# Moving a chunk's rows through DRAM ahead of the fetch of the next second weights, in a fused attention and mixture-of-experts kernel

## The chip, the cores and the metric

One core of one Trainium2 chip runs the whole kernel. The metric is the device time of one execution in microseconds (us); the times shown are medians of several runs on the chip. Durations come from one profiled execution of the kernel before.

## The reference

Linear attention with random features runs over 8 batches, 8 heads, 576 rows and 64 columns. Its output, read as 4608 tokens of 512 columns, goes into a mixture of 8 experts, of which each token uses one:

```python
def _moe_ref(x, w_gate, w1, w2):
    logits = x @ w_gate
    expert_idx = np.argmax(logits, axis=1)
    ...
    for e in range(E):
        mask = expert_idx == e
        ...
        h = np.maximum(x[mask] @ w1[e], 0.0)
        out[mask] = gate_w[mask, None] * (h @ w2[e])
```

`w1[e]` is 512 x 1024 and `w2[e]` is 1024 x 512, in float32, so each is 2 MB.

## The kernel before, in words

The attention takes the first 260 us or so of the span, and the change does not touch it. It leaves the token rows in DRAM (`token_rows`). What follows, and what this study is about, is the experts' part (class `Experts`).

**Chunks.** The tokens are sorted by expert into chunks of up to 384 (`T3`), each with tokens of one expert only. `plan` (L754) works out the chunks on the device and leaves them in `flags`: row 0 says that chunk t begins a new expert, row 1 which expert's weights come next, row 2 that chunk t exists, row 4 how many tokens it holds. Engines load these into registers and branch on them. Chunks 0 to 11 always run (`run`, L1215), later ones only if they exist (`tail`, L1159). In the profiled execution chunks 0 to 12 run, and chunks 4, 7 and 9 begin a new expert.

**One chunk** (`step`, L1136). Layer 1 (`layer1`, L1047) makes the hidden values in four groups g = 0 to 3 of two blocks each. TensorE (PE) multiplies into one of two PSUM pairs, `p_1[g % 2]`, and ScalarE (ACT) and VectorE (DVE) empty the pair into a high and a low part (L1001, L1002). PE can be two groups ahead of them and no more. A chunk of over 192 tokens takes the path of L975, a smaller one the path of L982 and L984, whose groups are about half as long. Layer 2 (`layer2`, L1064) multiplies by the second weights (L887, L1036), and the result is scaled and scattered to the output by GpSimd (POOL, L1083).

**How a chunk's rows arrive.** POOL gathers the rows of chunk t + 3 into `xg` or `xgm` (by parity of the chunk) during step t (L924). `move(t)` (L938), on the queue of SyncE (SP), writes them to a DRAM scratch `chunk_rows` (L943) and, when that has landed, reads them back with four transfers into `xq` in another order (L945). There is one `xq`. `xrows(t)` then turns `xq` into the chunk's transposed rows, three times a transpose on DVE (L952), a cast on ACT (L57) and a subtraction on DVE (L51).

**The order of the work.** It is written out by hand, and each engine works through its own share in that order. `begin(t)` (L1127) stands at the end of step t - 1, after its layers. In it SP does `move(t + 1)`, then `change(t, 1)`: if chunk t begins a new expert, ACT and DVE split the first weights `w1s` into `w1h` and `w1l`, and SP fetches the next expert's first weights into `w1s` (L904) once the split has read the old ones. After that DVE and ACT do `xrows(t + 1)`, if chunk t - 1 held over 192 tokens; otherwise it comes in the middle of layer 1 of chunk t, after group g = 1 (L1058 to L1062). The stores of the chunk's outputs by ACT stand behind `begin`.

The second weights are treated in the same way, within layer 1. In a chunk that begins a new expert each group first splits a quarter of `w2s`, and at the last group SP fetches the next expert's second weights (L907):

```python
for g in range(self.NF // 2):
    def fresh():
        self.split(2, (2 * g, 2 * g + 1))
        if g == self.NF // 2 - 1:
            self.next(t, 2)
    self.when(self.new, fresh)
```

So SP's order is `move(t + 1)`, `change(t, 1)`, `next(t, 2)` in the layer 1 of chunk t, `move(t + 2)`, and so on. The fetch for chunk 0 is unconditional and stands in step 0 (L1143).

Of the kernel before, what the change touches and what calls it, by code (L numbers as in the profile page):

```python
# [44 lines left out]
ET = mybir.EngineType  # L45
# [371 lines left out]
class Routing:  # L417
# [99 lines left out]
    def step(self, name, product, f):  # L517

        v = {}
        def made(bank):  # L520
            v["o"] = product(bank)
        def step():
            if "o" not in v:
                made(self.bank(name))
            f(v["o"])
        step.product = made
        return step
# [263 lines left out]
class Experts:  # L791
# [228 lines left out]
    def wide(self, t, g, n):  # L1020
        for f in (2 * g, 2 * g + 1):
            self.l1(t, f, n)
        self.hid(g, n)
# [17 lines left out]
    def load(self, t):  # L1041
        self.before = self.r2
        self.r1, self.r2, self.r3, self.r4 = (self.reg(4, t, T3, e) for e in (
            self.CE, (ET.Activation, ET.DVE), (ET.Activation, ET.DVE, ET.Pool), (ET.PE,)))
        self.new = self.reg(0, t, 1, self.WE)

    def layer1(self, t):  # L1047
        r = self.r1
        for g in range(self.NF // 2):
            def fresh():  # L1050
                self.split(2, (2 * g, 2 * g + 1))
                if g == self.NF // 2 - 1:
                    self.next(t, 2)
            self.when(self.new, fresh)
            wide = lambda n: lambda: self.wide(t, g, n)
            self.either(r > T2, lambda: self.either(r > T3 - HT, wide(T3), wide(T3 - HT)),
                        lambda: self.either(r > T2 - HT, wide(T2), lambda: self.slim(t, g)))
            if g == 1 and t == 1:  # L1058
                self.xrows(t + 1)
            elif g == 1:  # L1060
                with self.tc.If(self.before < T2 - HT + 1):  # L1061
                    self.xrows(t + 1)  # L1062
# [64 lines left out]
    def begin(self, t):  # L1127

        if t + 1 < NCH:
            self.move(t + 1)  # L1130
        self.change(t, 1)
        if 1 < t < NCH - 1:
            with self.tc.If(self.r2 > T2 - HT):
                self.xrows(t + 1)

    def step(self, t, following):  # L1136
        if t == 0:
            self.first(T3)
            self.l21()
            self.load(t)  # L1140
            self.xrows(1)
            self.gather(2)
            self.next(0, 2)  # L1143
        else:
            self.layer1(t)
        self.layer2(t)
        if t + 1 < NCH:
            self.weigh(t + 1)
        if t + 3 < NCH:
            self.gather(t + 3)  # L1150
        self.nc.gpsimd.drain()
        following()
        r, r2 = self.r3, self.r2
        if t + 1 < NCH:
            self.load(t + 1)
        for a in range(A3 - 1, -1, -1):
            self.out2(t, a, r, r2)
# [108 lines left out]
```

## Time and profile before

| | before |
|---|---|
| median of 3 runs | 710.49 us (709.24 to 710.63) |
| the profiled execution: time | 712.33 us |
| the profiled execution: span of its instructions | 710.6 us |
| mean granted TensorE clock, share of full speed | 0.974 |
| PE busy | 665.6 us (94% of the span) |
| DVE, ACT, POOL busy | 53%, 51%, 38% |
| moved by DMA | 100.51 MB, mean 141 GB/s |

The page counts an engine as busy while it works on data. Waiting, branching and issuing transfers do not count. A row of the timeline gives the start in us, the duration in us, the engine, the line of the kernel, the operation with its output and input, how many were merged into the row, and in brackets the idle time of the engine before it and what ended that. SPq marks instructions that SP itself executes, such as the issue of a transfer; the transfer lands later.

### The profile page before, as it was taken

To read this page: it belongs to the slowest core of one execution; us is meant where nothing else is said; L and a number is where in the kernel's file an instruction comes from. 1 tells how busy PE (TensorE), PEld (TensorE's weight loads), DVE (VectorE), ACT (ScalarE), POOL (GpSimd) and SP (SyncE) were. 2 spreads that over 40 slices of the span, in tenths; PEclk is the share of its full clock that TensorE was granted. 3 is DMA by queue.
4 is the path that set the end of the run, shared out by engine and by line. 5 is a ranking of instruction groups with operands and counts; after the bars stand their busy time and mean duration, and the time that the engine had idled before them with its cause. 6 is when DMAs were issued, how large, how long until landed. Compare 5 with 4: busy or idle time off the path is not lost. (4 is left out here: it accounts for less than half of the span.)

```text
span 710.6 us, 19585 instructions
## 1 busy us (share of the span) xinstructions
PE 665.6 (94%) x7011; PEld 604.4 (85%) x7011; DVE 377.2 (53%) x729; ACT 359.2 (51%) x1082; POOL 271.3 (38%) x492
## 2 busy tenths in 40 slices
PE   8999999999999999999999999599999499869994
PEld 5999999999888879898989898589898398768984
DVE  5788888888877787415132641231641355223222
ACT  5999999999989654212222530221530353122121
POOL 6545557777877762421313030313030221031212
PEclk9999999999999999999999999799999799979999
DMA  7782653844862227755244346324337253532200
GB/s 217 208 259 76 204 177 105 261 126 149 257 236 72 71 77 205 257 185 150 70 129 102 140 156 181 96 79 107 145 117 221 82 181 93 180 92 76 63 33 24
DMA packets 93105, 100.51 MB, mean 141 GB/s; under 512 B 28942, under 2 KB 73486, under 8 KB 92304
## 3 DMA queue, kind: packets, MB, share of 16 engines
q1 hardware_dynamic: 85216, 79.27, 36.9%
q0 software_dynamic: 7040, 19.04, 8.6%
q8 instruction: 89, 1.46, 0.9%
q14 instruction: 72, 0.59, 0.3%
q10 hardware_dynamic: 688, 0.16, 0.1%
HBM read 72.92 MB, written 29.77 MB: 145 GB/s over the span
## 5 line engine op out<-in xcount | busy, mean ns | idle before, releaser
L975 PE MATMUL p<-xb,w1p 128*128 128x384 f32 (+1 forms) x1056 | 188.3, 338 | 15.9 <-ACTq L1061 15.9
L975 PEld LDWEIGHTS p<-xb,w1p 128*128 128x128 f32 x1056 | 185.9, 192 | 17.7 <-ACTq L1061 16.5
L1083 POOL DMA_INDIRECT out_dram<-ys,idx x38 | 38.2, 1004 | 302.8 <-DVEq L1073 172.7
L887 PE MATMUL p<-w2p,hb 128*128 128x512 f32 x552 | 127.1, 389 | 0.0
L887 PEld LDWEIGHTS p<-w2p,hb 128*128 128x128 f32 x552 | 103.6, 188 | 21.6
L1002 DVE SCALAR_TENSOR_TENSOR hb<-p,hb 128x768 fp32r<-128x768 f32 (+1 forms) x44 | 41.0, 933 | 145.6 <-ACTq L1114 73.1
L1001 ACT ACTIVATE hb<-p 128x768 fp32r<-128x768 f32 (+1 forms) x44 | 34.9, 793 | 108.5 <-PE p L975 100.4
L191 DVE TENSOR_REDUCE mx<-pp 128x8 f32<-128x1024 f32 x64 | 78.0, 1218 | 10.9 <-PE pp L185 9.5
L199 ACT ACTIVATE qp<-pp,mx 128x128 f32<-128x128 f32 x256 | 77.1, 434 | 0.0
L199 ACT ACTIVATE kp<-pp,mx 128x128 f32<-128x128 f32 x256 | 74.0, 383 | 5.3 <-DVE de L283 1.9
L185 PE MATMUL pp<-omt,th 64*128 64x128 f32 x1024 | 72.1, 281 | 0.0
L185 PEld LDWEIGHTS pp<-omt,th 64*128 64x128 f32 x1024 | 63.4, 191 | 0.0
L887 PE MATMUL p_1tr<-w2p,hb 128*128 128x512 f32 x240 | 57.0, 391 | 0.5 <-DVEq L1114 0.4
L211 POOL TENSOR_TENSOR k<-kp 128x256 f32<-128x256 f32 x64 | 46.7, 729 | 23.7 <-ACT kp L199 18.8
L887 PEld LDWEIGHTS p_1tr<-w2p,hb 128*128 128x128 f32 x240 | 44.8, 188 | 10.2 <-DVEq L1114 0.8
L57 ACT CAST xb<-xgm 128x512 fp32r<-128x512 f32 x21 | 13.0, 621 | 75.4 <-DVE xgm L952 72.7
L274 PE MATMUL nu<-kva,qt 128*64 128x73 f32 x1008 | 46.3, 233 | 0.5 <-issue 0.5
L176 DVE COPY th<-tr 128x512 f32<-128x512 f32 x63 | 43.3, 687 | 5.0 <-PE tr L168 3.2
L243 ACT COPY qt<-t 128x512 f32<-128x512 f32 x64 | 42.1, 657 | 2.2 <-PE t L168 1.8
L952 DVE STREAM_TRANSPOSE xgm<-xq 128x512 f32<-128x512 f32 x21 | 22.7, 1082 | 36.1 <-DMA xq<-chunk_rows 31.7
L274 PEld LDWEIGHTS nu<-kva,qt 128*64 128x64 f32 x1008 | 36.8, 136 | 4.9 <-issue 0.6
L225 PE MATMUL kf<-kp,v 128*64 128x128 f32 x512 | 39.8, 275 | 0.0
(387 smaller groups left out, 1071.0 us busy)
## 6 DMA issues: line engine op xcount, KB each, us to landing
w1s<-in_moe_w_dram SPq DMA_DIRECT2D x5, 2048.0 KB
w2s<-in_moe_w_dram SPq DMA_DIRECT2D x5, 2048.0 KB
xq<-chunk_rows SPq DMA_DIRECT2D x52, 192.0 KB
v<-in_v_dram SPq DMA_DIRECT2D x32, 256.0 KB
token_rows<-x SPq DMA_DIRECT2D x8, 1024.0 KB
k<-in_k_dram SPq DMA_DIRECT2D x31, 256.0 KB
q<-in_q_dram SPq DMA_DIRECT2D x31, 256.0 KB
chunk_rows<-xgm SPq DMA_DIRECT2D x7, 768.0 KB
```

Source lines behind the costliest of these rows:

```text
L176: self.nc.vector.tensor_copy(t.rearrange("p n (a t) -> p a n t", a=2), s[("tr", h)])
L185: nc.tensor.matmul(o[:, a, n, :], t[r, n, :], self.om[r], start=True, stop=True)
L191: self.nc.vector.tensor_reduce(out=mx, in_=s[("pp", h)], axis=AX.X, op=ALU.max, negate=True)
L199: self.nc.scalar.activation(o[:, j, :], p[:, a, 2 * n + i, :], AF.Exp, bias=mx[:, a, 2 * n + i:2 * n + i + 1])
L211: nc.gpsimd.tensor_tensor(out=k2, in0=kp[:, :2, :], in1=kp[:, 2:, :], op=ALU.add)
L225: nc.tensor.matmul(pkv[c * D:(c + 1) * D, :M], vv, kk, start=n < 2, stop=n > 2)
L243: self.nc.scalar.copy(qt.rearrange("p n (a t) -> p a n t", a=2), s[("t2", h)])
L274: nc.tensor.matmul(o[r, j, :], qt[:, j, r], kva[:, h if h >= 0 else 2 * j + a, :], start=True, stop=True)
L887: self.nc.tensor.matmul(p, x, w[:, c, :], start=c == 0 and x is h and w is self.w2h, stop=c == self.NF - 1 and x is l)
L975: self.nc.tensor.matmul(o, w[:, c, k], x[:, c, :], start=i == 0, stop=i == len(ops) - 1)
L1002: self.nc.vector.scalar_tensor_tensor(out=l, in0=p, scalar=0.0, in1=h.bitcast(F32), op0=ALU.max, op1=ALU.subtract)
L1083: self.nc.gpsimd.indirect_dma_start(out=self.out[:, :], in_=y, in_offset=None, bounds_check=NT - 1, out_offset=bass.IndirectOffsetOnAxis(a ...
```

## The change

`next(t, 2)` leaves layer 1, and `next(0, 2)` leaves step 0. Both now stand in `begin`, one chunk later in its count, between the move and the change of first weights. SP's order becomes `move(t + 1)`, `next(t - 1, 2)` if chunk t - 1 began a new expert, `change(t, 1)`. The split of the second weights in layer 1 is now branched on by ACT and DVE alone, and SP has a register of its own, `fetch`, for the same flag. For the last chunk of all there is no `begin` behind it, and so no fetch.

```diff
@@ load, layer1
-        self.new = self.reg(0, t, 1, self.WE)
+        self.new, self.fetch = self.reg(0, t, 1, (ET.DVE, ET.Activation)), self.reg(0, t, 1, (ET.SP,))
...
         for g in range(self.NF // 2):
-            def fresh():
-                self.split(2, (2 * g, 2 * g + 1))
-                if g == self.NF // 2 - 1:
-                    self.next(t, 2)
-            self.when(self.new, fresh)
+            self.when(self.new, lambda: self.split(2, (2 * g, 2 * g + 1)))
@@ begin
         if t + 1 < NCH:
             self.move(t + 1)
+        if t == 1:
+            self.next(0, 2)
+        else:
+            self.when(self.fetch, lambda: self.next(t - 1, 2))
         self.change(t, 1)
@@ step
             self.gather(2)
-            self.next(0, 2)
```

## Rows read from the trace of the kernel before

**Rows 1.** Waits of PE from 380 to 710 us: total, times, longest.

```profile
PE p L975 <- ACTq L1061: 15.9, 2, 8.5
PE p L982 <- DVEq L1114: 9.8, 1, 9.8
```

**Rows 2.** Busy time by stretch: layer 1 of chunks 5, 6, 8, 10, 12.

```profile
core 0: us, PE busy (x) PEld busy (x) DVE busy (x) ACT busy (x) POOL busy (x), PEclk, DMA share, GB/s
436.61:463.73 27.12, 19.71 (x98) 19.42 (x97) 8.04 (x9) 6.31 (x9) 6.48 (x9) 0.81 0.45 117
480.09:496.75 16.66, 16.66 (x97) 16.66 (x96) 2.87 (x3) 3.13 (x4) 5.08 (x8) 1.00 0.44 104
546.14:567.82 21.68, 11.26 (x65) 10.77 (x64) 8.71 (x15) 7.63 (x16) 3.28 (x6) 0.76 0.32 99
611.09:638.61 27.52, 19.04 (x97) 18.75 (x96) 8.05 (x9) 6.31 (x9) 5.48 (x8) 0.81 0.42 110
688.00:698.62 10.62, 9.66 (x66) 9.05 (x64) 2.55 (x6) 3.54 (x8) 4.43 (x7) 1.00 0.15 55
```

**Rows 3.** Timeline of PE: layer 1 of chunk 2, and of chunk 5.

```profile
341.23 16.83 PE L975 MATMUL p<-xb,w1p 128*128 128x384 f32 x96
...
436.61 8.51 PE L975 MATMUL p<-xb,w1p 128*128 128x384 f32 x48
452.53 11.36 PE L975 MATMUL p<-xb,w1p 128*128 128x384 f32 x48 [7.41 <-ACTq L1061]
463.73 5.64 PE L887 MATMUL p_1tr<-w2p,hb 128*128 128x512 f32 x24
```

**Rows 4.** Timeline of DVE, in order of time.

```profile
332.04 1.09 DVE L952 STREAM_TRANSPOSE xgm<-xq 128x512 f32<-128x512 f32 x1 [3.10 <-DMA xg<-token_rows,idx]
...
413.18 0.96 DVE L1002 SCALAR_TENSOR_TENSOR hb<-p,hb 128x768 fp32r<-128x768 f32 x1 [1.07 <-ACTq L1061]
...
439.80 1.08 DVE L952 STREAM_TRANSPOSE xg<-xq 128x512 f32<-128x512 f32 x1 [17.35 <-DMA xq<-chunk_rows]
...
452.76 0.96 DVE L1002 SCALAR_TENSOR_TENSOR hb<-p,hb 128x768 fp32r<-128x768 f32 x1 [0.39 <-ACTq L1061]
...
522.71 0.96 DVE L1002 SCALAR_TENSOR_TENSOR hb<-p,hb 128x768 fp32r<-128x768 f32 x1 [1.87 <-ACTq L1061]
...
547.48 1.10 DVE L952 STREAM_TRANSPOSE xgm<-xq 128x512 f32<-128x512 f32 x1 [15.49 <-DMA xq<-chunk_rows]
...
594.13 0.69 DVE L51 TENSOR_TENSOR xb<-xg,xb 128x512 fp32r<-128x512 f32 x1 [0.73 <-ACT xb L57]
...
615.35 1.08 DVE L952 STREAM_TRANSPOSE xgm<-xq 128x512 f32<-128x512 f32 x1 [16.24 <-DMA xq<-chunk_rows]
```

**Rows 5.** Timeline of SP: issues of transfers, in order of time.

```profile
285.57 0.41 SPq L907 DMA_DIRECT2D w2s<-in_moe_w_dram  x1
...
306.21 2.99 SPq L945 DMA_DIRECT2D xq<-chunk_rows  x4
311.75 0.39 SPq L943 DMA_DIRECT2D chunk_rows<-xgm  x1
324.50 1.87 SPq L945 DMA_DIRECT2D xq<-chunk_rows  x4
...
397.25 0.37 SPq L904 DMA_DIRECT2D w1s<-in_moe_w_dram  x1
419.52 0.41 SPq L907 DMA_DIRECT2D w2s<-in_moe_w_dram  x1
420.29 0.38 SPq L943 DMA_DIRECT2D chunk_rows<-xg  x1
433.59 1.87 SPq L945 DMA_DIRECT2D xq<-chunk_rows  x4
...
453.81 2.15 SPq L945 DMA_DIRECT2D xq<-chunk_rows  x4
```

**Rows 6.** Waits of SP from 285 to 345 us: total, times, longest.

```profile
SPq L945 <- DVE xg L952: 9.0, 1, 9.0
```

## The prediction, made before the result was known

> **What bounds the kernel now.** I first read the waits of PE in the experts' part, because PE is busy nearly throughout and only its gaps can be won. Three gaps hold almost everything: two at L975 with 15.9 us together and one at L982 with 9.8 us [rows 1]. Next I took layer 1 of the chunks with a gap (5, 8 and 10) beside layer 1 of a chunk of the same path without one (6 for the wide path, 12 for the narrow) [rows 2]. The reader is to compare length, PE busy and granted clock. Chunk 5 takes 27.12 us where chunk 6 takes 16.66, and its PE is busy 19.71 us with the same 96 matmuls. So it lost 7.41 us of standing still and another 3.05 us because the matmuls ran slower. The timeline shows these within the layer: the first 48 matmuls take 8.51 us, then come 7.41 us of idleness, then the second 48 take 11.36 us [rows 3]. The granted clock of that stretch is 0.81; in chunk 6, where PE never stood, it is 1.00, which is 2.4 GHz [rows 2].
>
> Why PE stood is read on DVE. It waited 17.35 us until 439.80 for `xq`, and the second and third gaps have the same wait in front of them, 15.49 us until 547.48 and 16.24 us until 615.35 [rows 4]. The emptying of PSUM stands behind this work in DVE's and ACT's order, so PE fills both pairs and stops. How early `xq` must be there follows from the gaps. In chunk 5 it came 439.80 - 436.61 = 3.19 us after the layer's first matmul and cost 7.41 us, so it would have cost nothing if it had come 4.2 us before that matmul. Chunk 10 gives 615.35 - 611.09 = 4.26 us for 8.48 us (27.52 less 19.04), again 4.2 us. In chunk 8, with its shorter groups, 547.48 - 546.14 = 1.34 us cost 9.8, so 8.5 us [rows 1, 2, 4].
>
> Why `xq` was late is read on SP. After the fetch of first weights at 397.25 it does nothing until 419.52: `next(4, 2)` waits there for the last split of second weights, and the move of chunk 6 stands behind it. Its write goes out at 420.29, right behind a fetch of 2 MB, and lands after 13.3 us, at 433.59; the reads take 6.2 us more, to 439.80 [rows 4, 5]. The two other gaps follow a chunk that began a new expert in the same way.
>
> **The change part by part.**
>
> *The move goes ahead of the fetch.* SP reaches the write of chunk 6 after the fetch of first weights at 397.25; between a move's reads and the next write it spent 311.75 - 306.21 - 2.99 = 2.6 us on registers and branches, so I put the write at 400. It now lies behind a 2 MB fetch of first weights; by the 13.3 us above it lands by 413.6 at the latest. The reads have one more condition: `xq` must be free, and as `xrows(5)` stands in one of two places, SP hears of it only when DVE has passed group 1 of layer 1 of chunk 4. The trace of the next move shows this: reads at 453.81, right after DVE's L1002 at 452.76 + 0.96 = 453.72 [rows 4, 5]. In chunk 4 the same point is 413.18 + 0.96 = 414.1. So the rows land at 414.1 + 6.2 = 420.3, before DVE asks for them at 439.80 - 17.35 = 422.45, and 12.1 us before the 432.4 at which PE would notice. The move of chunk 9 is released at 522.71 + 0.96 = 523.7, lands at 529.9 and is needed at 547.48 - 9.8 = 537.7, 7.8 us in hand. That of chunk 11 is released when DVE ends `xrows(10)`, at 594.13 + 0.69 = 594.8, lands at 601.0 and is needed at 606.9, 5.9 us in hand [rows 2, 4]. (Within each chunk these distances stay the same when earlier gaps close.) The three gaps go. What they are worth comes from [rows 2]: chunk 5 less chunk 6, 27.12 - 16.66 = 10.46; chunk 10 less chunk 6, 27.52 - 16.66 = 10.86; chunk 8 less chunk 12, 21.68 - 10.62 = 11.06. **Sum: 32.4 us.** Of this 25.4 us is standing (7.41 + 8.48, and 10.42 - 0.96) and 7.0 us the slower matmuls.
>
> *The reads at risk.* The fetch now follows the reads by 3 to 5 us, and no row shows reads with a fetch right behind them. At best they take the 6.2 us of the reads at 433.59; at worst I give them the 13.3 us of the write behind a fetch. That lands them at 427.4, 537.0 and 608.1: only the last is late, by 1.2 us. I take 6.2, since they are ahead of the fetch on SP's queue, and keep 1.2 us for the range.
>
> *The first fetch moves most.* It goes from 285.57 to behind the reads of chunk 2, 306.21 + 2.99 = 309.2, just ahead of the write of chunk 3 at 311.75 [rows 5]. That write had 9.0 us in hand before its reads went out at 324.50 [rows 6]. Behind the fetch it lands by 311.75 + 13.3 = 325.1, 0.6 us late, and `xq` comes at 332.7 instead of 332.04; layer 1 of chunk 2 starts at 341.23 and needs it by 337.0 [rows 3, 4]. Cost zero, covered by 4.3 us. Without that cover each us late is a us of PE.
>
> *The other fetches* stay where they were, since the last split still releases them at 419.52 and SP has its reads out by 414.1 + 1.9. What waits for the weights is far away: the first fetch, now at 309.2, serves chunk 4, whose second weights are split only after 397.25 [rows 5]. The change of first weights stays behind them in SP's order as before. SP's lost branches and its extra register cost nothing: it waits for other engines nearly all the time. At the end of the kernel nothing changes.
>
> The profiled execution took 712.33 us, 1.7 us more than its span of 710.6, so the sum gives 712.33 - 32.4 = 679.9. It was 1.8 us above the median of 710.49, from which I subtract instead: **678.1 us**.
>
> **The rivals.**
>
> *A gap remains, or a new one opens in chunk 2.* For it: the margins of chunks 8 and 10 rest on a read time without a fetch, and the first fetch leaves its old place. Against it: 4 to 12 us in hand at each place. A gap kept whole costs up to 11.1 us: 678.1 + 11 = 689.
>
> *The gaps go, the slow matmuls stay.* Only the standing of 25.4 us is won, and the time is 685.1. For it: PE pauses in other places too, if for under a microsecond. Against it: chunk 6 changes PSUM pairs four times in its layer 1 at a granted 1.00 [rows 2]. The Trainium skill, in TensorE: Matmul & The Clock Gate, "A second HAM failure mode: psum-queue depth-cycling", says that short pauses between groups that cycle through PSUM banks can keep throttling the clock and releasing it again. By that rule this rival would hold; chunk 6's row speaks against it here.
>
> *The gaps move on by one chunk, and the kernel is slower.* The fetch now stands ahead of the move after next, so rows of chunks 3, 7, 10 and 12 could come late, four gaps in place of three: 4 x 10.8 - 32.4 = 10.8 us more, 721.3. It decides where a write behind the fetch takes longer than the reads' own wait for DVE. Against it: that wait is 9.0 us in chunk 3's move [rows 6], and in chunk 7's the reads go out only at 453.81, or some 7 us earlier without the gap, 27 us after the fetch [rows 5].
>
> *The change does not do what it says.* If the gather of chunk 6 were not there by 397, or the reads were released only with the last split, the write or the reads would go out as late as before: 710.5. Against it: a write at 397 instead of 420 has 23 us, and even reads released at 422.45 land at 428.7, before 432.4.
>
> **How the numbers follow.** All three gaps closed: 0.82. One kept or opened: 0.08. Slow matmuls stay: 0.04. Nothing: 0.03. Slower: 0.03. The first three are faster, 0.94. A measurement of this kernel can tell about 0.2%, or 1.4 us, from no change. The range runs from the lowest run before less the sum and a microsecond of smaller waits, 709.24 - 32.4 - 1.3 = 675.5, say 675, to one gap kept, 689; it takes in the 1.2 us of the reads and the slow-matmul case.
>
> **What would show it.** Right: layer 1 of chunks 5 and 10 at 16.7 us and of chunk 8 at about 10.6, granted clock 1.00 in them; no wait of DVE for `xq` over 3 us; on SP the reads of chunks 6, 9 and 11 ahead of the fetch of second weights; the first such fetch some 23 us later than before. Wrong: a wait of PE at L975 or L982 over 2 us, above all in chunk 2, or a write that lands later than DVE passes group 1.

## The result and the profile after

The changed kernel takes 678.96 us (median of 4 runs, 678.77 to 679.88); the kernel before, beside it, 709.9 us (709.24 to 710.63). The ratio is 0.9567, with a 95% interval of 0.955 to 0.9583, so the change is faster by 4.3%. The forecast was 678.1 us. The profiled execution took 679.88 us (its span is 678.2 us), 32.45 us less than the 712.33 us of the profiled execution before; the sum in the prediction said 32.4. Between the medians it is 30.9 us, because the profiled execution of the kernel before lay 1.8 to 2.4 us above its median and the one after only 0.9 us.

The waits of PE in the experts' part come first, as in [rows 1]. Here they are for 380 to 679 us of the changed kernel (line numbers are each kernel's own: L1061 and L1114 of before are L1057 and L1110 here):

```profile
PE p L1036 <- PEq L1064: 1.5, 2, 0.9
PE p_1tr L887 <- DVEq L1110: 0.5, 1, 0.5
PE p L982 <- issue: 0.3, 1, 0.3
```

The two entries of 15.9 and 9.8 us are gone. Nothing above a microsecond took their place. The busy time by stretch answers to [rows 2], with the same columns; the stretches are again layer 1 of chunks 5, 6, 8, 10 and 12, at their new times:

```profile
435.83:452.49 16.66, 16.66 (x97) 16.66 (x96) 2.87 (x3) 3.13 (x4) 5.47 (x8) 1.00 0.41 97
468.86:485.52 16.66, 16.66 (x97) 16.66 (x96) 2.87 (x3) 3.13 (x4) 5.46 (x8) 1.00 0.42 102
534.91:545.33 10.42, 9.64 (x66) 9.07 (x64) 3.55 (x9) 4.45 (x11) 4.54 (x7) 1.00 0.38 106
588.74:605.40 16.66, 16.66 (x97) 16.66 (x96) 2.87 (x3) 3.13 (x4) 5.47 (x8) 1.00 0.36 97
654.79:665.61 10.82, 9.66 (x66) 9.05 (x64) 2.62 (x6) 3.44 (x8) 4.47 (x7) 1.00 0.15 55
```

Chunks 5 and 10 are now as long as chunk 6, and the granted clock is 1.00 in all five, where it was 0.81, 0.76 and 0.81 in the three with gaps. The starts of these stretches, set beside those of [rows 2], tell where the time went: 0.8 us less before chunk 5, 10.45 us between the starts of chunks 5 and 6, 11.1 us between those of chunks 8 and 10, 10.9 us between those of chunks 10 and 12. That is 33.2 us, of which the last layers and the end gave back 0.8.

SP's issues and DVE's rows answer to [rows 5] and [rows 4]. SP first:

```profile
309.04 0.40 SPq L907 DMA_DIRECT2D w2s<-in_moe_w_dram  x1
311.52 0.39 SPq L943 DMA_DIRECT2D chunk_rows<-xgm  x1
323.41 2.20 SPq L945 DMA_DIRECT2D xq<-chunk_rows  x4
...
395.97 0.38 SPq L904 DMA_DIRECT2D w1s<-in_moe_w_dram  x1
397.30 0.39 SPq L943 DMA_DIRECT2D chunk_rows<-xg  x1
413.05 2.03 SPq L945 DMA_DIRECT2D xq<-chunk_rows  x4
418.86 0.39 SPq L907 DMA_DIRECT2D w2s<-in_moe_w_dram  x1
...
512.52 2.58 SPq L945 DMA_DIRECT2D xq<-chunk_rows  x4
...
570.98 2.04 SPq L945 DMA_DIRECT2D xq<-chunk_rows  x4
```

The write of chunk 6 leaves at 397.30 in place of 420.29, and its reads are out before the fetch. DVE's side, with the first transpose of chunks 3, 6, 9 and 11 and two rows that release reads:

```profile
331.26 1.08 DVE L952 STREAM_TRANSPOSE xgm<-xq 128x512 f32<-128x512 f32 x1 [3.42 <-DMA xq<-chunk_rows]
...
412.01 0.95 DVE L1002 SCALAR_TENSOR_TENSOR hb<-p,hb 128x768 fp32r<-128x768 f32 x1
...
422.16 1.09 DVE L952 STREAM_TRANSPOSE xg<-xq 128x512 f32<-128x512 f32 x1 [0.49 <-DVEq L1110]
...
521.40 1.08 DVE L952 STREAM_TRANSPOSE xgm<-xq 128x512 f32<-128x512 f32 x1 [0.64 <-DMA xg<-token_rows,idx]
...
569.87 1.09 DVE L952 STREAM_TRANSPOSE xg<-xq 128x512 f32<-128x512 f32 x1
...
577.56 1.10 DVE L952 STREAM_TRANSPOSE xgm<-xq 128x512 f32<-128x512 f32 x1 [0.80 <-DMA xg<-token_rows,idx]
```

In place of the waits of 17.35, 15.49 and 16.24 us for `xq`, DVE was idle for 0.49, 0.64 and 0.80 us before the rows of chunks 6, 9 and 11, and the profile puts none of the three down to `xq`. A wait for `xq` of 3.42 us is left before the rows of chunk 3, ahead of the stretch with the gaps.

### The profile page after: what moved, and what is told of

It reads as the page before. It is cut to its first block, busy times and chain, and to the rows that moved or that the text cites. A ratio compares the mean times of both kernels' runs of the same rounds, so it can differ in the third digit from the quotient of the medians.

```text
span 678.2 us, 19569 instructions
## 1 busy us (share of the span) xinstructions
PE 658.5 (97%) x7011; PEld 597.8 (88%) x7011; DVE 376.7 (56%) x729; ACT 359.2 (53%) x1082; POOL 271.4 (40%) x492
## 5 line engine op out<-in xcount | busy, mean ns | idle before, releaser
L975 PE MATMUL p<-xb,w1p 128*128 128x384 f32 (+1 forms) x1056 | 183.4, 333 | 0.5 <-DVE xb L51 0.4
L975 PEld LDWEIGHTS p<-xb,w1p 128*128 128x128 f32 x1056 | 181.0, 188 | 2.3 <-issue 1.5
L1002 DVE SCALAR_TENSOR_TENSOR hb<-p,hb 128x768 fp32r<-128x768 f32 (+1 forms) x44 | 41.0, 932 | 154.5 <-ACTq L1110 96.3
L924 POOL DMA_INDIRECT xg<-token_rows,idx x24 | 26.4, 1100 | 30.2 <-DVEq L1110 17.3
```

Of the source, the lines that this page charges most:

```text
L975: self.nc.tensor.matmul(o, w[:, c, k], x[:, c, :], start=i == 0, stop=i == len(ops) - 1)
L1002: self.nc.vector.scalar_tensor_tensor(out=l, in0=p, scalar=0.0, in1=h.bitcast(F32), op0=ALU.max, op1=ALU.subtract)
```

## The experiments

**Order alone.** The changed kernel, with the fetch put ahead of the move again:

```diff
@@ begin
-        if t + 1 < NCH:
-            self.move(t + 1)
         if t == 1:
             self.next(0, 2)
         else:
             self.when(self.fetch, lambda: self.next(t - 1, 2))
+        if t + 1 < NCH:
+            self.move(t + 1)
```

> The changed kernel with one edit: in begin the fetch of the next second weights stands ahead of the move again, as it did in the kernel before; the fetch stays out of layer 1, and SP keeps its own register. Theory (the order of move and fetch on SP is all of the gain): the write of chunk 6 goes out behind the fetch at about 420 us again, all three gaps come back with about 10.5, 11 and 10.9 us, and the time is 709 to 711.5 us. Rival (the gain comes from SP being out of the branches of layer 1, or from the first fetch being later): the time stays near 679 us and no wait of PE over 2 us comes back.

Measured: 710.87 us (709.14 to 713.22), ratio to the kernel before 0.9989, interval 0.9965 to 1.0013. The waits of PE from 380 to 710 us:

```profile
PE p L975 <- ACTq L1057: 17.1, 2, 9.5
PE p L982 <- DVEq L1110: 9.6, 1, 9.6
```

and the second half of layer 1 of chunk 10:

```profile
625.77 9.98 PE L975 MATMUL p<-xb,w1p 128*128 128x384 f32 x48 [9.54 <-ACTq L1057]
```

All three gaps are back, so the order of move and fetch on SP is the whole of the gain. Taking SP out of the branches of layer 1 gains nothing that this can measure.

**The first fetch alone.** The changed kernel, with the unconditional fetch back in step 0:

```diff
@@ begin
-        if t == 1:
-            self.next(0, 2)
-        else:
+        if t > 1:
             self.when(self.fetch, lambda: self.next(t - 1, 2))
@@ step
             self.gather(2)
+            self.next(0, 2)
```

> The changed kernel with one edit: the first fetch of second weights, the unconditional one, goes back to step 0, to about 285 us; the three later ones stay behind the moves. Theory (the first fetch has nothing to do with the gain and its new place costs nothing): within 1.4 us of the changed kernel, 677.6 to 680.4 us, and the write of chunk 3 lands some 7 us earlier than in the changed kernel, so that its reads wait for DVE for 9 us again in place of 0.7. Rival (the first fetch in its new place, beside gathers and the write of chunk 3, costs the experts' part something): faster than the changed kernel by over 1.4 us.

Measured: 679.18 us (678.14 to 679.67) beside 678.96 for the changed kernel. The new place costs nothing and brings nothing. What it takes is slack: from 300 to 330 us SP's reads of chunk 3 waited for DVE for 9.3 us here, and 0.7 us in the changed kernel, of whose waits in that stretch these two belong to the reads of chunk 3:

```profile
SPq L945 <- DMA chunk_rows<-xgm: 10.7, 1, 10.7
SPq L945 <- DVE xg L952: 0.7, 1, 0.7
```

Of the 11.5 us between write and reads of chunk 3, 10.7 were now the landing of the write behind the fetch. The reads still went out on time.

**A small fetch: an experiment that missed its aim.** The kernel before, with a later fetch that brings only the first eighth:

```diff
@@ next
-        (self.dma1 if n == 1 else self.dma2)(bass.ds(e, 1))
+        if n == 2 and t > 0:
+            self.nc.sync.dma_start(self.w2s[:, :1], ...[:, :1])
+        else:
+            (self.dma1 if n == 1 else self.dma2)(bass.ds(e, 1))
```

> The kernel before with one edit: the second weights' fetches of chunks 4, 7 and 9 bring an eighth of the weights (256 KB instead of 2 MB), so that later experts use old second weights for the rest; order and waits on SP stay as before. It parts what the gap is made of: SP's in-order wait for the split keeps the write back until about 420, 529.8 and 599.0 us, but hardly anything lies ahead of it then. Theory (wait and traffic are both needed): the write lands in about 4 us, the rows 6.2 us later, at 430.5, 540 and 609.3; against 432.4, 537.7 and 606.9 that is no gap in chunk 5 and gaps of 2 to 3 us in chunks 8 and 10, with at most 3 us of slower matmuls: 683 to 689 us. Rival A (the wait on SP alone makes the gaps): three gaps of 7 to 10 us as before, 705 to 711 us. Rival B (the traffic alone): no gap, 677 to 681 us.

Measured: 678.52 us (677.89 to 678.73), as fast as the changed kernel. But the edit took away more than traffic. A fetch of the first eighth has to wait only for the first split, and it left at 408.76 where the full one left at 419.52 [rows 5]; so SP's wait was shorter too, and the run parts nothing. The next two were made to part it.

**The wait without the traffic.** The same, with the last eighth, which is split last:

```diff
-            self.nc.sync.dma_start(self.w2s[:, :1], ...[:, :1])
+            self.nc.sync.dma_start(self.w2s[:, 7:], ...[:, 7:])
```

> The kernel before with one edit: the second weights' fetches of chunks 4, 7 and 9 bring the last eighth of the weights alone (256 KB), the one that is split last, so that later experts use old second weights for the rest. The run with the first eighth did not part wait and traffic, since it had to wait only for the first split and went out 11 us earlier; this one waits for the last split as the full fetch does, and so holds the write back until about 420 (chunk 6), 530 (chunk 9) and 599 us (chunk 11) in the times of the kernel before, with hardly any traffic ahead of it. Theory (wait and traffic are both needed): the write lands in 3 to 4.5 us, the rows 6.2 us later, at 429.5 to 431, 539 to 540.5 and 608.4 to 609.7; against the limits 432.4, 537.7 and 606.9 there is no gap in chunk 5 and gaps of 1.3 to 2.8 us in chunks 8 and 10, with up to 3 us of slower matmuls each: 681 to 689 us. Rival A (the wait on SP alone makes the gaps): 705 to 711. Rival B (the traffic alone): 677 to 680.

Measured: 691.26 us (690.47 to 692.09), 2 us above the expected range. PE's timeline of layer 1 of chunks 5, 8 and 10:

```profile
434.95 8.51 PE L975 MATMUL p<-xb,w1p 128*128 128x384 f32 x48
444.80 8.65 PE L975 MATMUL p<-xb,w1p 128*128 128x384 f32 x48 [1.33 <-ACTq L1061]
...
546.06 0.66 PE L982 MATMUL p<-xb,w1p 128*128 128x384 f32 x1 [5.64 <-DVEq L1114]
...
597.71 8.51 PE L975 MATMUL p<-xb,w1p 128*128 128x384 f32 x48
608.75 8.59 PE L975 MATMUL p<-xb,w1p 128*128 128x384 f32 x48 [2.53 <-ACTq L1061]
```

and DVE's, when the rows of chunks 6, 9 and 11 came:

```profile
432.06 1.09 DVE L952 STREAM_TRANSPOSE xg<-xq 128x512 f32<-128x512 f32 x1 [11.26 <-DMA xq<-chunk_rows]
...
532.54 1.09 DVE L952 STREAM_TRANSPOSE xgm<-xq 128x512 f32<-128x512 f32 x1 [11.00 <-DMA xq<-chunk_rows]
...
596.03 1.08 DVE L952 STREAM_TRANSPOSE xgm<-xq 128x512 f32<-128x512 f32 x1 [10.29 <-DMA xq<-chunk_rows]
```

The fetch left 19.5 us after SP began to wait, as in the kernel before, and the gaps shrank to 1.33, 5.64 and 2.53 us. The expected landing was too early: the write of chunk 6 left at 418.60 and was there by 425.81, 7.2 us and not 3 to 4.5, and for chunk 9 the write took 5.6 us and the reads 7.4, which made the gap of 5.64 us in chunk 8, expected at 1.3 to 2.8.

**The traffic without the wait.** The small, early fetch again, and behind it a copy of the 2 MB to a spare place in DRAM:

```diff
@@ next
         if n == 2 and t > 0:
             self.nc.sync.dma_start(self.w2s[:, :1], ...[:, :1])
+            self.nc.sync.dma_start(self.spare, ...)
```

> The kernel before with one edit: the second weights' fetches of chunks 4, 7 and 9 bring the first eighth alone (later experts use old second weights for the rest), which releases SP some 11 us earlier, and right behind it SP copies the 2 MB of those weights from DRAM to a spare place in DRAM. So 2 MB of traffic stand ahead of the move's write as in the kernel before, without the long wait of SP. Theory (both are needed): the write goes out at about 410, 506 and 560 us, lands within 13.3 us, the rows are there by 429.7, 525.6 and 579.4 against limits of about 432, 526.8 and 584.5, and there is no gap over 1 us: 678 to 682 us. Rival B (the traffic alone makes the gaps): three gaps of 7 us and more, over 700 us.

Measured: 682.25 us (681.52 to 683.1), with two gaps where at most 1 us was expected; the rows of chunk 6 came 10.4 us after the first read went out (423.09 to 433.45), and not 6.2. The waits of PE from 380 to 682 us:

```profile
PE p L976 <- ACTq L1062: 1.6, 1, 1.6
PE p L983 <- DVEq L1115: 1.5, 1, 1.5
```

So the full wait with an eighth of the traffic costs 691.26 - 678.96 = 12.3 us, the traffic with the shorter wait 3.3 us, and both together 31 to 32. Each uses up slack that the other needs. The shares are not quite pure: SP still waited 9.4 us for the first split in this run (19.5 us for the last split in the run before it), and the copy goes from DRAM to DRAM and is not the same traffic as a fetch, so the 3.3 is only near to the fetch's own share.

**The fetch between write and reads.** The changed kernel, with the fetch inside the move:

```diff
@@ move
-    def move(self, t):
+    def move(self, t, between=None):
...
+        between()
         for q in range(4):
```

> The changed kernel with one edit: in begin the fetch of second weights stands between the move's write and its four reads, so the write still goes out early and only the reads lie behind 2 MB. This measures the risk that the prediction kept for the range (reads with a fetch at their side) and the limits of 4.2 and 8.5 us. Theory: reads go out at about 419, 518.5 and 576.5 us and land 11 to 13.3 us later, at 430 to 432.6, 529.5 to 532 and 587.5 to 590; the limits in the changed kernel's times are 431.6, 526.4 and 584.5, so chunk 5 loses 0 to 1 us, chunks 8 and 10 lose 3 to 5.5 each, chunk 1 0 to 1.5, and slower matmuls add 0 to 2 us per gap: 685 to 695 us. Rival (the write's place alone matters, the reads overtake or share with the fetch): within 2 us of 679.

Measured: 700.79 us (699.64 to 703.11): the direction is the theory's, the size is not. The issues on SP, DVE's first transposes of chunks 6, 9 and 11, and PE where it went on after its gaps in chunks 5, 8 and 10:

```profile
419.20 0.39 SPq L907 DMA_DIRECT2D w2s<-in_moe_w_dram  x1
419.96 7.80 SPq L947 DMA_DIRECT2D xq<-chunk_rows  x4
...
525.88 5.40 SPq L947 DMA_DIRECT2D xq<-chunk_rows  x4
...
592.66 4.32 SPq L947 DMA_DIRECT2D xq<-chunk_rows  x4
```

```profile
436.99 1.11 DVE L954 STREAM_TRANSPOSE xg<-xq 128x512 f32<-128x512 f32 x1 [14.95 <-DMA xq<-chunk_rows]
...
539.55 1.09 DVE L954 STREAM_TRANSPOSE xgm<-xq 128x512 f32<-128x512 f32 x1 [11.59 <-DMA xq<-chunk_rows]
...
604.99 1.11 DVE L954 STREAM_TRANSPOSE xgm<-xq 128x512 f32<-128x512 f32 x1 [12.36 <-DMA xq<-chunk_rows]
```

```profile
449.71 10.15 PE L977 MATMUL p<-xb,w1p 128*128 128x384 f32 x48 [5.00 <-ACTq L1059]
...
552.76 0.66 PE L984 MATMUL p<-xb,w1p 128*128 128x384 f32 x1 [5.92 <-DVEq L1112]
...
617.75 11.42 PE L977 MATMUL p<-xb,w1p 128*128 128x384 f32 x48 [4.62 <-ACTq L1059]
```

The reads of chunk 6 went out 6.9 us later than in the changed kernel (413.05), because the fetch ahead of them waits for the last split. Behind the fetch the rows came 17.0, 13.7 and 12.3 us after the first read, against 6.2 in [rows 4, 5]. Part of it lies on SP: the four issues took 7.8, 5.4 and 4.3 us, where they take 2.0 to 2.6 in the changed kernel's rows above. PE stood for 5.00, 5.92 and 4.62 us, and the granted clock of these three layers was 0.93, 0.73 and 0.86, so 70% of the gain was lost (21.8 of 30.9 us). It is the reads' place ahead of the fetch that counts, and the early write alone is not enough.

**A double dose.** The changed kernel, with each fetch of second weights issued twice:

```diff
@@ next
-        (self.dma1 if n == 1 else self.dma2)(bass.ds(e, 1))
+        for _ in range(n):
+            (self.dma1 if n == 1 else self.dma2)(bass.ds(e, 1))
```

> The changed kernel with one edit: each fetch of second weights is issued twice in a row, so that 4 MB, and SP's wait for the first of the two to land, stand ahead of the next move. It tests the rival of the prediction that the gaps move on by one chunk, at a higher dose. Theory: only chunk 3's rows have so little in hand that it shows: second fetch at about 320 us, write of chunk 3 at 322.5, landed at 333 to 334, rows at 339.5 against a limit of 340.8 - 4.2 = 336.6, so layer 1 of chunk 2 loses about 3 to 4 us and some slower matmuls; the moves of chunks 7, 10 and 12 wait for DVE longer than that (14.8, 9.4 and 21.2 us in the changed kernel) and lose nothing: 682 to 687 us. Rival (the gaps move on whenever a fetch is ahead of the next rows): gaps in layer 1 of chunks 6, 9 and 11 as well, 700 us or more.

Measured: 686.78 us (684.34 to 690.48). DVE's first transpose of chunk 3, and PE's timeline of layer 1 of chunk 2:

```profile
343.12 1.10 DVE L952 STREAM_TRANSPOSE xgm<-xq 128x512 f32<-128x512 f32 x1 [13.05 <-DMA xq<-chunk_rows]
```

```profile
342.38 8.51 PE L975 MATMUL p<-xb,w1p 128*128 128x384 f32 x48
355.71 11.25 PE L975 MATMUL p<-xb,w1p 128*128 128x384 f32 x48 [4.82 <-ACTq L1057]
```

One gap of 4.8 us, in chunk 2 as expected (3 to 4 us), and none in layer 1 of chunks 6, 9 and 11. The gaps do move on by one chunk where the next rows have no slack; with one fetch no place has so little.

## Why the prediction was right

**The bound.** The gaps were the bound: with them gone PE is busy 658.5 us of 678.2, or 97%, and the rest of the program kept its pace. Between the profiled executions the sum of 32.4 us holds chunk by chunk. The forecast took it from the median before, and lies 0.9 us too low because that profiled execution was slower than its median by more than the one after.

**How early `xq` must come.** The 4.2 us was worked out from two gaps, and the experiments test it on others. In the run with the fetch between, chunk 5 started at 436.19 and chunk 10 at 604.62, the rows came 0.80 and 0.37 us later, and PE stood 5.00 and 4.62 us. With the small last fetch they came 2.89 and 1.68 us before the start, for 1.33 and 2.53 us. With the double dose, 0.74 us after, for 4.82. Standing time less lateness is 4.20, 4.25, 4.22, 4.21 and 4.08. The 8.5 us of chunk 8 was worked out from one gap alone. There the same sum gives 5.92 + 2.56 = 8.48 with the fetch between, where the layer started at 542.11, and 5.64 + 3.15 = 8.79 with the small last fetch, where it started at 535.69.

**The release of the reads.** SP issued chunk 6's reads at 413.05, 0.1 us after DVE's L1002 ended at 412.01 + 0.95; the prediction had 414.1 for DVE's times of before, with the program since running about 1 us ahead. The changed kernel's waits of SP from 390 to 420 us show the order of the two conditions:

```profile
SPq L945 <- DMA chunk_rows<-xg: 8.5, 1, 8.5
...
SPq L945 <- DVEq L1057: 6.8, 1, 6.8
```

The write behind the fetch of first weights landed after 8.5 us, well under the 13.3 allowed, and the reads then waited 6.8 us for DVE. The reads of chunks 9 and 11 came out at 512.52 and 570.98. The prediction's 523.7 and 594.8, less the 11.2 and 22.4 us by which the program now runs ahead there, give 512.5 and 572.4. For chunk 11 it named the wrong release: not the last subtraction of `xrows(10)`, but its last transpose, the last to read `xq`, which ended at 569.87 + 1.09 = 570.96. The 1.4 us only added to the time in hand.

**The first fetch.** Forecast at 309.2, issued at 309.04. The write of chunk 3 was given until 325.1 and landed at 311.9 + 10.7 = 322.6; `xq` came at 331.26, with 5.3 us to the limit of 340.77 - 4.2. One sign that the prediction had named did not come: DVE's wait for `xq` there is 3.42 us, and it had said none over 3. It cost nothing, by the same 5.3 us.

**The clock.** The 7.0 us of slower matmuls were won together with the gaps: PE is busy 658.5 us where it was 665.6, with as many matmuls, and the granted clock is 1.00 in all five stretches. So the rival that keeps them fell. It is the one for which the prediction cited the Trainium skill (TensorE: Matmul & The Clock Gate, "A second HAM failure mode: psum-queue depth-cycling"), and this trace does not show that oscillation: in chunk 8 PE paused for 0.78 us of its 10.42, in chunks 5, 6 and 10 not at all, and the granted clock stayed at 1.00.

**The reads at risk.** The prediction took 6.2 us for reads with a fetch right behind them and 13.3 us as the worst case, priced at 1.2 us. The changed kernel shows such reads itself. For chunks 6, 9 and 11 the fetch left 2.8 to 3.8 us after the last of the four reads had been issued. Here are these reads, with the time of one issue in ns, the first and last start in us, and the time of one read from issue to landing:

```profile
L945 SPq DMA_DIRECT2D xq<-chunk_rows x4: 317/496/591, 413.1 to 414.6; - x4
DMA to landing us min/median/max: 3.3/4.1/4.5
...
L945 SPq DMA_DIRECT2D xq<-chunk_rows x4: 317/468/1199, 512.5 to 514.6; - x4
DMA to landing us min/median/max: 3.8/5.0/5.8
...
L945 SPq DMA_DIRECT2D xq<-chunk_rows x4: 307/394/479, 571.0 to 572.7; - x4
DMA to landing us min/median/max: 3.0/4.2/4.7
```

So the rows were there by 419.1, 520.4 and 577.4, at most 6.1, 7.9 and 6.4 us after the first read. The 6.2 held but for 1.7 us in chunk 9, and the worst case did not come. The limits, 4.2, 8.5 and 4.2 us ahead of the starts of chunks 5, 8 and 10, are now 431.6, 526.4 and 584.5, so 12.5, 6.0 and 7.1 us were in hand, where the prediction had 12.1, 7.8 and 5.9. Reads behind a fetch, which the run with the fetch between made, are another matter: up to 17.0 us, and 22 us of time. The share of wait and traffic, which the prediction left undivided, is now known to within what was said of those two runs: 12.3 and 3.3 us apart, 31 to 32 together.

Not tried: the fetch on another engine's queue, which would take its wait for the split out of the move's way.

## What to carry to other kernels

On a queue that works in order, put what somebody waits for ahead of what waits for a release, and let a large transfer that nobody needs soon go last. Work out from the gaps how early a buffer must arrive, and compare each new arrival with that limit; here the same number then gave PE's standing time in every variant to within 0.3 us. A late transfer may need two causes together, so take them away one at a time before naming one.

## What the runs showed that was not expected

The cost of the slower clock did not grow with the standing time before it. After 4.62 and 5.00 us of standing the next 48 matmuls took 11.42 and 10.15 us with the fetch between, after 4.82 us 11.25 with the double dose, after 7.41 and 8.48 us 11.36 and 10.69 in the kernel before, after 7.57 and 9.54 us 10.60 and 9.98 with the order alone put back; undisturbed, 48 take 8.5. After 1.33 and 2.53 us they took 8.65 and 8.59 us, in stretches with a granted clock of 1.00. So these two short gaps of the small last fetch cost little more than their own length, and the longer ones 1.5 to 2.9 us more.

The second is SP's issue time. A read's issue takes at most 1.56 us in the changed kernel and took up to 5.06 us behind a fetch that had just been issued, in the run with the fetch between: a transfer can be late before it has left its queue. The write just behind a fetch was issued in 0.38 us [rows 5], so this did not strike every transfer there, and no run shows what the issue waits for.
